# Attention's probabilities turned in pairs of 64-row tiles, and a sign carried by two slopes

## The chip, the cores and the metric

One core of a Trainium2 chip runs one launch that computes attention and two MLP blocks. The metric is the device time of that launch in microseconds (us); the time of a kernel is the median of its runs. Engines: PE is TensorE (PEld its weight loads), DVE is VectorE, ACT is ScalarE, POOL is GpSimd, SP is SyncE, which issues the transfers.

## What is computed

Three stages for 4 batches of 576 tokens, 8 heads of 64 columns, model width 512. Inputs are float32, but the weight matrices of all stages but one (`w_sg`) come as float64.

```python
q_rot, k_rot = (rotate(q), rotate(k))
scores = scale * np.matmul(q_rot, k_rot.transpose(0, 1, 3, 2))
scores = scores - np.max(scores, axis=-1, keepdims=True)
attn = np.exp(scores)
attn = attn / (np.sum(attn, axis=-1, keepdims=True) + 1e-09)
x = np.matmul(attn, v)                      # heads side by side: (4, 576, 512)
xn = (x - mu) / np.sqrt(var + 1e-06) * g_ln # LN over 512
x = x + np.maximum(xn @ w_ch1, 0.0) @ w_ch2 # 512 -> 2048 -> 512
h = gelu(x @ w_in)                          # 512 -> 1024, u and v halves
v_s = np.einsum('ts,bsd->btd', w_sg, norm(v)) + b_sg
out = x + (u * v_s) @ w_out
```

## The kernel before

**Attention** (class `Attn`) goes through 32 blocks: 4 batches (groups `g` 0 to 3), 4 pairs of heads `p`, 2 spans `hi` of queries (0 to 383 and 384 to 575). Group 0 takes all first spans, then all second ones. A block has units of 128 queries for both heads of the pair (3 for span 0; for span 1 one, and one of 64 queries whose two heads share the 128 rows): 80 units, 64 of them full. A unit (`unit`) computes the scores of 576 keys per head: queries and keys of head j lie on partitions 64j to 64j + 63, so the two heads' matmuls use the two 64-row halves of TensorE's array (row tiles). Scores go to PSUM tiles S0 and S1, two banks each. VectorE takes each row's maximum (L293), ScalarE the exponential into `P` in SBUF with the row sums (L303). `turn` transposes `P` with 128x128 transposes (L334), three to a PSUM tile `T` of one bank (two such tiles, tag `T`), nine for a full unit and five for one of 64 queries; `evac` copies each tile into `PT` on ACT or DVE (L347; L352 and L356 for the unit of 64 queries). When a whole block is turned, `values` multiplies with v: one full-array matmul for the last 64 keys of both heads (L394) and eight with 64 output columns each, a pair on the two column halves of the array (column tiles, L398). Then the reciprocal row sums are transposed (L408), copied and multiplied in. PV, these reciprocals and the LN sums (L508) use the tag `T` too.

**MLP.** Each group's LN and MLP (`ln`, `rest`, `up`, `down`) run on TensorE in between the attention of later groups: rounded high and low words in fp32r, three matmuls of 288 columns per 128x128 block (L655 to L657 up, L685 to L687 down), PSUM tag `m` with two banks. The third stage (`moe2`, PSUM tag `p`) follows and is not touched.

**Weights.** `double_parts` turns 44 tiles of float64 (128x512) into float32: ACT scales the high word as a float (L54) and the low word (L56), DVE shifts and joins them (L58) and then joins in the sign bit (L60). `convert` (32 tiles of the first MLP) and `split` (12 of the third stage) call it.

**Order.** Within an engine the instructions stand in program order, and that is set by a planner (`Sched`): tasks name an engine, an earliest time and a duration; the one that could start first goes next, and one of a lower rank may go ahead if it could start within `HOLD` of the duration. Ranks (`UNIT`, `RANK`, `NORM`, `REST`) are tables by group, `EVEN` sets how copies are shared between ACT and DVE. Each engine runs its list in order, so a waiting instruction holds up all behind it.

Of the kernel before, what the change touches and what calls it, by code (L numbers as in the profile page):

```python
# [15 lines left out]
HQ = 288  # L16
# [6 lines left out]
HOLD = 0.2  # L23
UNIT = [2, 1, 3, 2.5]
EVEN = [0, 9, 3, -1]
RANK = dict(turn=4.5, evac=1.25, values=2.25, end=-1, convert=2.75, prep=3.5, load=4, loader=4)
NORM, REST = [2.25, 0, 3.5, 1.25], [0.25, 4.5, 1, 1]
# [15 lines left out]
def double_parts(nc, q, pool, src, bufs):  # L43
# [10 lines left out]
    nc.scalar.activation(f32(e), f32(H), AF.Copy, scale=2.0 ** -112)  # L54
# [4 lines left out]
    yield None  # L59
    nc.vector.scalar_tensor_tensor(e, H, -0x80000000, e, op0=ALU.bitwise_and, op1=ALU.bitwise_or)  # L60
# [3 lines left out]
class Sched:  # L64
# [7 lines left out]
    def __init__(self):  # L72
        self.e = dict.fromkeys(("PE", "DVE", "ACT", "POOL", "SP"), 0.0)
        self.tasks = []
        self.n = 0

# [6 lines left out]
    def go_on(self, t, end):  # L83
        try:
            t["eng"], t["at"], t["us"], *rank = t["gen"].send(end)
# [49 lines left out]
class Attn:  # L135
# [10 lines left out]
    def __init__(self, tc, ctx, k, groups, sched):  # L146
# [5 lines left out]
        self.T, self.qin, self.kin, self.vfree, self.K = Bank(2), Bank(QB), Bank(2), Bank(2), Bank(KB)  # L152
# [105 lines left out]
    def unit(self, i):  # L258
# [3 lines left out]
        x0 = (g, B["p"])  # L262

        heads = range(2 if m == 128 else 1)
        for n in range(2):
            yield "PE", (lambda: latest(*self.Sfree, Kb["k"], B["q"], self.k["x0_free"](*x0))) if n == 0 else 0.0, 0.57
# [5 lines left out]
            self.Sfree = [None, None]  # L272
        e = c.e["PE"]
        if u["t"] == 0:
            self.k["x0"](*x0)
        if u["last"]:
            self.qin.give(B["qslot"], e + 0.1)
            if B["hi"]:
                self.QD.give(B["dslot"], e + 0.1)
            Kb["kusers"] -= 1  # L280
            if Kb["kusers"] == 0:
                self.K.give(Kb["kslot"], e + 0.1)
        if i + 1 < len(self.units):
            c.task(self.unit(i + 1), UNIT[self.units[i + 1]["g"]])
        if u["t"] == 0:
            self.ahead(B["n"])
            B["su"] = self.p.tile([128, 6], F32, tag="su", name="su", bufs=3)
            B["left"] = 0
        at = []
        nb = self.p.tile([128, 2], F32, tag="nb", name="nb", bufs=3)  # L290
        for j in heads:
            e = yield "DVE", e + 0.35 if j == 0 else 0.0, 0.77
            nc.vector.tensor_reduce(nb[:, j:j + 1], S[j], AX.XY, ALU.max, negate=True)  # L293
            at.append(e + 0.1)
        P = None
        u["P"] = []
        for j in heads:
            e = yield "ACT", (lambda: latest(at[0], self.P.free())) if j == 0 else at[j], 0.97
            if j == 0:
                slot = self.P.take()  # L300
                P = self.p.tile([128, 1152], F32, tag="P", name="P", bufs=PB)
# [4 lines left out]
            if len(heads) == 1:  # L306
                self.Sfree[1] = e + 0.05
            if j == 0:
                c.task(self.turn(u, P, slot, at), RANK["turn"])
            if len(heads) == 1:  # L310
# [3 lines left out]
        if u["last"]:  # L314
            c.task(self.scale(B, e + 0.15), RANK["values"])

    def turn(self, u, P, slot, at):

        nc, c, B, q0, m = self.nc, self.c, u["B"], u["q0"], u["m"]
        full = m == 128  # L320
        for k in range(3 if full else 2):
            need = 1 if full and k else 0
            e = yield "PE", (lambda: latest(u["P"][need] if len(u["P"]) > need else None, self.T.free(),
                                            0.0 if B["pt"] else self.PT.free())), 0.39
# [3 lines left out]
            bank = self.T.take()  # L328
            ps = self.ps.tile([128, 512], F32, tag="T", name="T", bufs=2)
            for i in range(3 * k, 3 * k + 3):  # L330
                if not full and i > 4:
                    break
                n = i - 3 * k
                nc.tensor.transpose(ps[:, 128 * n:128 * n + 128], P[:, 128 * i:128 * i + 128], self.k["ident"])  # L334
            c.task(self.evac(u, k, ps, bank, e, full), RANK["evac"])
            B["left"] += 1
        self.P.give(slot, e + 0.1)
        u["turned"] = True

    def evac(self, u, k, ps, bank, e, full):  # L340
        nc, c, B, q0 = self.nc, self.c, u["B"], u["q0"]
# [3 lines left out]
        if full:  # L345
            e = yield eng, e + 0.35, 0.52
            copy(t[:, 3 * k:3 * k + 3, q0:q0 + 128], ps[:, 0:384].rearrange("p (c q) -> p c q", c=3))  # L347
        else:
            for j in range(2):
                a, n = 5 * j + 3 * k, (3, 1)[k]  # L350
                e = yield eng, e + 0.35 if j == 0 else 0.0, (0.33, 0.2)[k]
                copy(t[:, a:a + n, q0:q0 + 64], ps[:, 0:128 * n].rearrange("p (c j q) -> p c j q", c=n, j=2)[:, :, j, :])  # L352
            for j in range(2) if k else ():
                r = slice(64 * j, 64 * j + 64)
                e = yield eng, 0.0, 0.2
                copy(t[r, 4, q0:q0 + 64], ps[r, 128 + 64 * j:192 + 64 * j])  # L356
        self.T.give(bank, e + 0.1)
        B["left"] -= 1
        B["ready"] = max(B.get("ready", 0.0), e + 0.1)
        u["out"] = u.get("out", 0) + 1  # L360
        if u["last"] and u["out"] == 1:
            c.task(self.values(B, u), RANK["values"])
# [19 lines left out]
    def values(self, B, u):  # L382
# [5 lines left out]
        ready = lambda: B["ready"] if u.get("turned") and B["left"] == 0 else None  # L388
        for s in range(2):
            e = yield "PE", (lambda: latest(ready(), self.T.free(), V["v"])) if s == 0 else 0.0, 0.15 + 0.00168 * n * (3, 2)[s]  # L390
            if s == 0:
                bank = self.T.take()
                ps = self.ps.tile([128, 512], F32, tag="T", name="PV", bufs=2)
# [10 lines left out]
        f = yield "PE", lambda: latest(B.get("inv"), self.T.free()), 0.08 + 0.00087 * n  # L404
        b2 = self.T.take()
        pb = self.ps.tile([128, 512], F32, tag="T", name="inv", bufs=2)
# [4 lines left out]
        self.T.give(bank, e + 0.1)  # L411
# [8 lines left out]
        self.T.give(b2, e + 0.1)  # L420
# [21 lines left out]
def fused_kernel(ctx, tc, q, k, v, cs, cst, w12, wi, wo, wsg, wsg4, gb, out):  # L442
# [36 lines left out]

    attn_ctx = ExitStack()  # L480
# [650 lines left out]
```

## Time and profile before

| | |
|---|---|
| time, median of 3 runs | 948.84 us (948.66 to 951.78) |
| the profiled execution | 947.07 us, span 945.3 us |
| PE busy | 916.1 us, 97% |
| PEld busy | 799.5 us, 85% |
| DVE busy | 638.3 us, 68% |
| ACT busy | 490.9 us, 52% |
| chain that ended last | PE 93%, DVE 3%, ACT 2%, DMA 1%, issue 1% |
| granted TensorE clock over the span | 1.000 |

The profile is of one execution. Busy shares count an engine's instructions from start to end; TensorE's overlap, so what a matmul costs in a stream is read from the distance between starts. Attention's transposes lie between 15 and 539 us of the span; the first MLP matmul starts at 89.84 us.

### The profile page before, as it was taken

The page shows a single profiled execution, that of the slowest core. Times are in us where ns is not written, and L with a number is a line of the kernel's source. Part 1 is how long each engine was busy: PE and PEld are TensorE (multiplying, and loading weights), DVE is VectorE, ACT ScalarE, POOL GpSimd, SP SyncE. Part 2 cuts the span into 40 slices and gives each one's busy share as a digit, 9 for nine tenths or more (in the row PEclk, how much of TensorE's full clock was granted, in tenths as well). Part 3 has the DMA queues.
Part 4 walks back from the last instruction along what each step waited for, and adds up shares of the span by engine and source line. Part 5 has one row for each costly group of instructions (what it writes and reads, how often), then busy time and mean ns, then how long its engine had stood idle before and what let it go on. Part 6 is the DMA issues. An engine that isn't in the chain of part 4 may idle for free.

```text
span 945.3 us, 16622 instructions
## 1 busy us (share of the span) xinstructions
PE 916.1 (97%) x6448; PEld 799.5 (85%) x6448; DVE 638.3 (68%) x1353; ACT 490.9 (52%) x1191; POOL 0.8 (0%) x9
## 2 busy tenths in 40 slices
PE   4889999999999999999999999989999999999998
PEld 2446878788788787899877899989999999999998
DVE  6799887887869744825767423674534898676754
ACT  2688787778654755524255413444322656263530
POOL 0000000000000000000000000000000000000000
PEclk9999999999999999999999999999999999999999
DMA  6477616674536055225730453878752201202011
GB/s 205 167 239 242 218 43 199 220 249 172 201 110 206 18 182 182 84 74 184 230 114 22 131 163 98 304 238 295 247 190 80 84 1 31 83 1 88 1 51 51
DMA packets 57791, 134.69 MB, mean 142 GB/s; under 512 B 8048, under 2 KB 30448, under 8 KB 57712
## 3 DMA queue, kind: packets, MB, share of 16 engines
q1 hardware_dynamic: 56880, 132.96, 42.5%
q8 instruction: 51, 0.84, 0.4%
q10 hardware_dynamic: 832, 0.66, 0.3%
q14 instruction: 28, 0.23, 0.1%
HBM read 106.50 MB, written 26.21 MB: 140 GB/s over the span
## 4 chain that ended last, share of the span: by engine, by line
PE 93%; DVE 3%; ACT 2%; DMA 1%; issue 1%; SPq 0%; DVEq 0%
PE S L271 9%; PE T L334 8%; PE m L686 7%; PE m L685 7%; PE m L687 7%; PE m L655 7%; PE PV L398 7%; PE m L656 7%; PE m L657 7%; PE PV L394 2%; PE p L964 2%; PE p L962 2%; PE p L963 2%; PE p L1062 2%; PE p L1046 2%; PE p L1061 2%
## 5 line engine op out<-in xcount | busy, mean ns | idle before, releaser
L655 PE MATMUL m<-xh,w 128*128 128x288 f32 x480 | 147.1, 306 | 3.5 <-DVE h L665 3.5
L685 PE MATMUL m<-h,w 128*128 128x288 f32 x480 | 146.0, 304 | 0.0
L686 PE MATMUL m<-h,w 128*128 128x288 f32 x480 | 141.8, 295 | 0.0
L656 PE MATMUL m<-xl,w 128*128 128x288 f32 x480 | 141.6, 295 | 0.0
L657 PE MATMUL m<-xh,w 128*128 128x288 f32 x480 | 141.2, 294 | 0.0
L687 PE MATMUL m<-h,w 128*128 128x288 f32 x480 | 140.5, 293 | 0.0
L303 ACT ACTIVATE P<-S,nb 128x576 f32<-128x576 f32 x144 | 106.4, 744 | 42.4 <-DVE nb L293 39.3
L665 DVE SCALAR_TENSOR_TENSOR h<-m,h 128x288 fp32r<-128x288 f32 x128 | 58.1, 455 | 100.5 <-ACT h L663 99.4
L293 DVE TENSOR_REDUCE nb<-S 128x1 f32<-128x576 f32 x144 | 103.6, 752 | 26.4 <-PE S L271 25.8
L334 PE MATMUL T<-ident,P 128*128 128x128 f32 x656 | 100.1, 280 | 9.0 <-ACT P L303 4.9
L347 ACT COPY PT<-T 128x384 f32<-128x384 f32 x157 | 70.7, 483 | 69.4 <-PE T L334 69.2
L334 PEld LDWEIGHTS T<-ident,P 128*128 128x128 f32 x656 | 74.9, 141 | 37.3 <-issue 12.7
L663 ACT ACTIVATE h<-m 128x288 fp32r<-128x288 f32 x128 | 52.5, 410 | 100.2 <-PE m L657 98.7
L271 PE MATMUL S<-K,qin 64*128 64x288 f32 x512 | 85.2, 439 | 11.0 <-DVE K L205 11.0
L655 PEld LDWEIGHTS m<-xh,w 128*128 128x128 f32 x480 | 90.1, 188 | 5.8 <-DVE h L665 4.2
L685 PEld LDWEIGHTS m<-h,w 128*128 128x128 f32 x480 | 90.1, 188 | 0.8 <-DVE acc L709 0.4
L686 PEld LDWEIGHTS m<-h,w 128*128 128x128 f32 x480 | 90.4, 188 | 0.4
L656 PEld LDWEIGHTS m<-xl,w 128*128 128x128 f32 x480 | 90.3, 188 | 0.2
L657 PEld LDWEIGHTS m<-xh,w 128*128 128x128 f32 x480 | 90.3, 188 | 0.0
L687 PEld LDWEIGHTS m<-h,w 128*128 128x128 f32 x480 | 90.1, 188 | 0.0
L271 PEld LDWEIGHTS S<-K,qin 64*128 64x128 f32 x512 | 47.7, 190 | 31.1 <-DVE K L205 11.0
L398 PE MATMUL PV<-PT,vin 128*64 128x384 f32 (+1 forms) x512 | 70.3, 413 | 0.0
(148 smaller groups left out, 1797.3 us busy)
## 6 DMA issues: line engine op xcount, KB each, us to landing
w<-wsc SPq DMA_DIRECT2D x96, 512.0 KB, 4.0
cd<-in_w SPq DMA_DIRECT2D x32, 512.0 KB, 4.3
wsc<-w SPq DMA_DIRECT2D x24, 512.0 KB, 4.2
kin<-in_k SPq DMA_DIRECT2D x15, 576.0 KB, 5.9
vin<-in_v SPq DMA_DIRECT2D x20, 320.0 KB, 3.9
qin<-in_q SPq DMA_DIRECT2D x16, 384.0 KB, 5.2
x1d<-x SPq DMA_DIRECT2D x32, 144.0 KB, 3.3
x<-x1d SPq DMA_DIRECT2D x32, 144.0 KB, 2.8
```

The source lines that it names most:

```text
L271: nc.tensor.matmul(S[j][:, n, :], q, Kb["K"][r, a:a + HQ], start=True, stop=True)
L293: nc.vector.tensor_reduce(nb[:, j:j + 1], S[j], AX.XY, ALU.max, negate=True)
L303: nc.scalar.activation(P[:, 576 * j:576 * j + 576].rearrange("p (n k) -> p n k", n=2), S[j], AF.Exp, bias=nb[:, j:j + 1], scale=1.0, accum ...
L334: nc.tensor.transpose(ps[:, 128 * n:128 * n + 128], P[:, 128 * i:128 * i + 128], self.k["ident"])
L347: copy(t[:, 3 * k:3 * k + 3, q0:q0 + 128], ps[:, 0:384].rearrange("p (c q) -> p c q", c=3))
L398: nc.tensor.matmul(ps[r, 0:n], V["vin"][:, ch, r], t[:, 5 * j + ch, 0:n], start=False, stop=ch == 3, skip_group_check=True)
L655: nc.tensor.matmul(ps, w[:, 0, ms], xh[:, kc, :], start=kc == 0, stop=False)
L656: nc.tensor.matmul(ps, w[:, 0, ms], xl[:, kc, :], start=False, stop=False)
L657: nc.tensor.matmul(ps, w[:, 1, ms], xh[:, kc, :], start=False, stop=kc == 3)
L685: nc.tensor.matmul(ps, w[:, 0, ms], t[:, 0, :], start=a == 0, stop=False)
L686: nc.tensor.matmul(ps, w[:, 1, ms], t[:, 0, :], start=False, stop=False)
L687: nc.tensor.matmul(ps, w[:, 0, ms], t[:, 1, :], start=False, stop=a == n - 1)
```

## The change

- **Transposes.** `turn` works on a block's list of 64-row by 128-key pieces: for each 128 keys of a unit it issues two transposes of 64 queries, one on each row half of the array, into the two banks of one PSUM tile `T` (`[128, 2, 512]`, one such tile in place of two small ones). Eight such pairs fill it (four and five in the blocks `ALONE`); a group may span units. `evac` copies a unit's part of a group in one instruction.
- **Scores.** In the blocks `ALONE` (batch 0, first span, four blocks) a unit is done for head 0, then for head 1, each waiting for its own S tile only.
- **Values.** The fifth chunk (last 64 keys) becomes a column pair like the others; PV and the reciprocals share one `T`, and in batch 0's first span use `m`'s PSUM tiles. The LN sums get 128 output columns in place of 64.
- **Sign.** ACT's pass over the high word is Prelu with scale 2^-112 for positive words and 2^-112 times 2^32 for negative ones: the shift by three puts that power on the sign bit. DVE's sign step goes, 44 times.
- **Planner.** It adds `SWITCH` when TensorE's tiling changes; the tables of ranks are others.

```diff
@@
-HOLD = 0.2
...
+HOLD = 0.3
+SWITCH = 0.2
+ALONE = ((0, 0),)
...
@@
-    nc.scalar.activation(f32(e), f32(H), AF.Copy, scale=2.0 ** -112)
+    nc.scalar.activation(f32(e), f32(H), AF.Prelu, scale=2.0 ** -112, alpha=2.0 ** 32)
...
     nc.vector.scalar_tensor_tensor(e, e, 3, d[:, :, 0], op0=ALU.logical_shift_left, op1=ALU.bitwise_or)
-    yield None
-    nc.vector.scalar_tensor_tensor(e, H, -0x80000000, e, op0=ALU.bitwise_and, op1=ALU.bitwise_or)
     yield f32(e)
@@
+            if t["eng"] == "PE":
+                if t["mode"] != self.mode:
+                    t["us"] += SWITCH
+                self.mode = t["mode"]
@@
-    def turn(self, u, P, slot, at):
...
-            bank = self.T.take()
-            ps = self.ps.tile([128, 512], F32, tag="T", name="T", bufs=2)
-            for i in range(3 * k, 3 * k + 3):
...
-                nc.tensor.transpose(ps[:, 128 * n:128 * n + 128], P[:, 128 * i:128 * i + 128], self.k["ident"])
+    def turn(self, B, units):
...
+        blocks = [(u, i) for u in units for i in range(9 if u["m"] == 128 else 5)]
...
+            cuts.append(min(cuts[-1] + (8 if (B["g"], B["hi"]) not in ALONE else 5 if i or u["m"] < 128 else 4), len(blocks)))
...
+            self.T.take()
+            ps = self.ps.tile([128, 2, 512], F32, tag="T", name="T")
...
+            for n, (x, i) in enumerate(some):
+                for j in range(2):
+                    r = slice(64 * j, 64 * j + 64)
+                    nc.tensor.transpose(ps[:, j, 64 * n:64 * n + 64], x["tile"][r, 128 * i:128 * i + 128], self.k["ident"][r, r])
@@
-            copy(t[:, 3 * k:3 * k + 3, q0:q0 + 128], ps[:, 0:384].rearrange("p (c q) -> p c q", c=3))
+                copy(t[:, i:i + n, q0:q0 + 128].rearrange("p c (j q) -> p j c q", j=2),
+                     ps[:, :, 64 * s:64 * s + 64 * n].rearrange("p j (c q) -> p j c q", q=64))
@@
-                nc.tensor.matmul(ps[:, 0:n], V["vin"][:, 4, :], t[:, 4, 0:n], start=True, stop=False, skip_group_check=True)
-            for ch in (2 * s, 2 * s + 1):
...
+            for ch in chs:
                 for j in range(2):
                     r = slice(64 * j, 64 * j + 64)
-                    nc.tensor.matmul(ps[r, 0:n], V["vin"][:, ch, r], t[:, 5 * j + ch, 0:n], start=False, stop=ch == 3, skip_group_check=True)
+                    nc.tensor.matmul(ps[r, 0:n], V["vin"][:, ch, r], t[:, 4 if ch == 4 else 5 * j + ch, 0:n], start=ch == 0, stop=ch == 4)
@@
-            nc.tensor.matmul(ps, ones[:, 0:m], x, start=i == 0, stop=i == len(xs) - 1)
+            nc.tensor.matmul(ps, ones, x, start=i == 0, stop=i == len(xs) - 1)
```

How TensorE's list begins, before (S_79 and S_80 are the two heads' score tiles; a row with x3 stands for three instructions):

```order
L271 MATMUL S_79<-K,qin 128x288
L271 MATMUL S_80<-K,qin 128x288
L271 MATMUL S_79<-K,qin 128x288
L271 MATMUL S_80<-K,qin 128x288
L334 MATMUL T<-ident,P 128x128 x3
L271 MATMUL S_79<-K,qin 128x288
L271 MATMUL S_80<-K,qin 128x288
```

and now:

```order
L281 MATMUL S_79<-K,qin 128x288 x2
L281 MATMUL S_80<-K,qin 128x288 x2
L281 MATMUL S_79<-K,qin 128x288 x2
L281 MATMUL S_80<-K,qin 128x288 x2
L353 MATMUL T<-ident,P 128x64 x8
L281 MATMUL S_79<-K,qin 128x288 x2
L353 MATMUL T<-ident,P 128x64 x10
```

The two heads no longer alternate: a head's two matmuls stand together, and its transposes follow in groups of four and five pairs.

TensorE in the middle of the MLP (m) of group 0, beside the attention of group 1, before:

```order
L657 MATMUL m<-xh,wx 128x288
L271 MATMUL S_79<-K,qin 128x288
L271 MATMUL S_80<-K,qin 128x288
L271 MATMUL S_79<-K,qin 128x288
L271 MATMUL S_80<-K,qin 128x288
L334 MATMUL T<-ident,P 128x128 x6
L655 MATMUL m<-xh,wx 128x288
L656 MATMUL m<-xl,wx 128x288
L657 MATMUL m<-xh,wx 128x288
```

and now, at about the same place:

```order
L281 MATMUL S_79<-K,qin 128x288
L281 MATMUL S_80<-K,qin 128x288
L281 MATMUL S_79<-K,qin 128x288
L281 MATMUL S_80<-K,qin 128x288
L726 MATMUL m<-h,w 128x288
L727 MATMUL m<-h,w 128x288
L728 MATMUL m<-h,w 128x288
L726 MATMUL m<-h,w 128x288
L727 MATMUL m<-h,w 128x288
L728 MATMUL m<-h,w 128x288
L353 MATMUL T<-ident,P 128x64 x12
L726 MATMUL m<-h,w 128x288
```

Six transposes stood right behind the scores, on the full array like the MLP; now the scores are followed by the MLP, and six pairs of transposes (x12) stand by themselves between MLP matmuls.

## Rows read from the trace of the kernel before

**Rows 1.** The table by stretches: busy us and instructions by engine, clock, DMA.

```profile
core 0: us, PE busy (x) PEld busy (x) DVE busy (x) ACT busy (x) POOL busy (x), PEclk, DMA share, GB/s
11.00:90.00 79.00, 68.53 (x380) 40.56 (x381) 69.58 (x138) 57.25 (x136) 0.00 (x0) 1.00 0.59 197
90.00:525.00 435.00, 433.58 (x3134) 360.52 (x3134) 314.68 (x659) 262.32 (x675) 0.00 (x0) 1.00 0.45 151
```

**Rows 2.** The timeline, PE: start, us, engine, line, operation, out<-in, shapes, count.

```profile
89.26 0.82 PE L334 MATMUL T<-ident,P 128*128 128x128 f32 x6
89.84 0.38 PE L655 MATMUL m<-xh,w 128*128 128x288 f32 x1
90.05 0.29 PE L656 MATMUL m<-xl,w 128*128 128x288 f32 x1
...
90.58 0.29 PE L657 MATMUL m<-xh,w 128*128 128x288 f32 x1
```

**Rows 3.** The timeline, PE, 101.1 to 103.4 us: scores and transposes between MLP matmuls.

```profile
101.18 0.29 PE L657 MATMUL m<-xh,w 128*128 128x288 f32 x1
101.41 1.24 PE L271 MATMUL S<-K,qin 64*128 64x288 f32 x8
102.58 0.77 PE L334 MATMUL T<-ident,P 128*128 128x128 f32 x5
103.10 0.38 PE L685 MATMUL m<-h,w 128*128 128x288 f32 x1
103.31 0.29 PE L686 MATMUL m<-h,w 128*128 128x288 f32 x1
```

**Rows 4.** The timeline, PE, 95.2 to 97.4 us: the values of a block.

```profile
95.24 0.48 PE L394 MATMUL PV<-PT,vin 128*128 128x192 f32 x2
95.65 1.52 PE L398 MATMUL PV<-PT,vin 128*64 128x192 f32 x16
97.10 0.44 PE L408 MATMUL inv<-ident,rb 128*128 128x128 f32 x2
97.38 1.14 PE L271 MATMUL S<-K,qd 128*128 128x288 f32 x4
```

**Rows 5.** The timeline, PE, of two ever longer stretches: score passes merged.

```profile
301.88 0.76 PE L271 MATMUL S<-K,qin 64*128 64x288 f32 x4
301.88 1.00 PE L271 MATMUL S<-K,qin 64*128 64x288 f32 x6
```

**Rows 6.** The timeline, PEld, of short stretches: weight loads merged, scores' and transposes'.

```profile
301.88 0.19 PEld L271 LDWEIGHTS S<-K,qin 64*128 64x128 f32 x2 [0.17 <-issue]
301.88 0.30 PEld L271 LDWEIGHTS S<-K,qin 64*128 64x128 f32 x4 [0.17 <-issue]
303.05 0.20 PEld L334 LDWEIGHTS T<-ident,P 128*128 128x128 f32 x2 [0.39 <-issue]
```

**Rows 7.** The timeline, PEld and PE, of short stretches from 53.3 us on.

```profile
53.38 0.14 PEld L334 LDWEIGHTS T<-ident,P 128*128 128x128 f32 x1 [0.22 <-ACT P L303]
53.41 0.30 PE L334 MATMUL T<-ident,P 128*128 128x128 f32 x1
53.38 0.20 PEld L334 LDWEIGHTS T<-ident,P 128*128 128x128 f32 x2 [0.22 <-ACT P L303]
```

**Rows 8.** The timeline, 38.9 to 46 us: a unit of the first stage.

```profile
39.03 1.47 PE L271 MATMUL S<-K,qin 64*128 64x288 f32 x8
...
40.31 1.41 DVE L293 TENSOR_REDUCE nb<-S 128x1 f32<-128x576 f32 x2
...
41.55 0.55 PE L334 MATMUL T<-ident,P 128*128 128x128 f32 x3 [0.24 <-ACT PT L347]
...
42.84 0.77 ACT L303 ACTIVATE P<-S,nb 128x576 f32<-128x576 f32 x1
```

**Rows 9.** Groups by line: count, busy us, mean ns, idle us before, releasers.

```profile
L334 PE MATMUL T<-ident,P 128*128 128x128 f32 x656 | 100.1, 280 | 9.0 <-ACT P L303 4.9 <-DVE PT L347 2.2 <-ACT PT L347 1.5
L60 DVE SCALAR_TENSOR_TENSOR ce<-cd,ce 128x512 int32<-128x512 int32 x44 | 30.3, 688 | 0.8
L347 ACT COPY PT<-T 128x384 f32<-128x384 f32 x157 | 70.7, 483 | 69.4 <-PE T L334 69.2
```

More of the change, by code (lines that the diff above doesn't have):

```diff
@@ L22 @@
 L_CONV = 10.0
-HOLD = 0.2
[L24 to L27, printed above, removed]
+HOLD = 0.3
+SWITCH = 0.2
+ALONE = ((0, 0),)
+UNIT = [0.5, 2, 2.75, 4]
+EVEN = [3, 3, -3, 3]
+RANK = dict(end=-1, convert=2.75, prep=2.75, load=4.5, loader=0.75)
+NORM, REST = [-1, 1, 2.25, 1], [1.75, 0.75, 1.5, 4.5]
+TURN, EVAC, VAL = [0.75, 1.5, 0, 2.75], [0.25, 0, 1.75, 3.5], [1.75, -1, 2.25, 3]
 FG = [4, 8, 8, 4]
@@ L256, in load_v, with unit @@
             self.c.task(v_task(), RANK["load"] + 0.02 * bi)
-    def unit(self, i):
+    def unit(self, i, heads=None):
         nc, c, u = self.nc, self.c, self.units[i]
@@ L262, in unit @@
         x0 = (g, B["p"])
-        heads = range(2 if m == 128 else 1)
+        if heads is None:
+            heads = (0, 1) if m == 128 and (g, B["hi"]) not in ALONE else (0,)
+        single = m == 64
         for n in range(2):
-            yield "PE", (lambda: latest(*self.Sfree, Kb["k"], B["q"], self.k["x0_free"](*x0))) if n == 0 else 0.0, 0.57
+            yield "PE" if single else "PEr", (lambda: latest(*(self.Sfree[j] for j in ((0, 1) if single and (g, B["hi"]) not in ALONE else heads)), Kb["k"], B["q"],
+                                                             self.k["x0_free"](*x0))) if n == 0 else 0.0, 0.49
             for j in heads:
@@ L283, in unit @@
[L283 to L290, printed above, removed]
+        if heads[0] == 0:
+            if u["t"] == 0:
+                self.k["x0"](*x0)
+                self.ahead(B["n"])
+                B["su"] = self.p.tile([128, 6], F32, tag="su", name="su", bufs=3)
+                B["left"] = 0
+                B["turned"] = False
+            u["P"], u["at"] = [], []
+            u["nb"] = self.p.tile([128, 2], F32, tag="nb", name="nb", bufs=3)
@@ new lines, in unit @@
+        after = single or heads[-1] == 1
+        if not after:
+            c.task(self.unit(i, (1,)), UNIT[g])
+        if after:
+            if u["last"]:
+                self.qin.give(B["qslot"], e + 0.1)
+                if B["hi"]:
+                    self.QD.give(B["dslot"], e + 0.1)
+                Kb["kusers"] -= 1
+                if Kb["kusers"] == 0:
+                    self.K.give(Kb["kslot"], e + 0.1)
+            if i + 1 < len(self.units):
+                c.task(self.unit(i + 1), UNIT[self.units[i + 1]["g"]])
@@ L305, in unit @@
             self.Sfree[j] = e + 0.05
[L306 to L310, printed above, removed]
+            if j == 0 and u["t"] == 0:
+                c.task(self.turn(B, [x for x in self.units if x["B"] is B]), TURN[B["g"]])
+            if single:
                 e = yield "ACT", 0.0, 0.2
@@ L313, in unit @@
             u["P"].append(e + 0.15)
-        if u["last"]:
-            c.task(self.scale(B, e + 0.15), RANK["values"])
-    def turn(self, u, P, slot, at):
[L319 to L324, printed above, removed]
+        if after and u["last"]:
+            c.task(self.scale(B, e + 0.15), VAL[B["g"]])
+    def turn(self, B, units):
+        nc, c = self.nc, self.c
+        blocks = [(u, i) for u in units for i in range(9 if u["m"] == 128 else 5)]
+        cuts = [0]
+        while cuts[-1] < len(blocks):
+            u, i = blocks[cuts[-1]]
+            cuts.append(min(cuts[-1] + (8 if (B["g"], B["hi"]) not in ALONE else 5 if i or u["m"] < 128 else 4), len(blocks)))
+        for v, z in zip(cuts, cuts[1:]):
+            some = blocks[v:z]
+            u, i = some[-1]
+            need = 1 if u["m"] == 128 and i > 3 else 0
+            e = yield "PEr", lambda: latest(u["P"][need] if len(u.get("P", ())) > need else None, self.T.free(),
+                                            0.0 if B["pt"] else self.PT.free()), 0.06 * len(some)
             if not B["pt"]:
@@ L555, in rest @@
         r = G[g, "r"]
-        nc.scalar.copy(r[a:a + m], ps)
+        nc.scalar.copy(r[a:a + m], ps[a:a + m])
         mpsb.give(bank, e + 0.05)
@@ L627, in convert @@
         next(parts)
-        yield "DVE", e + 0.1, 0.7
-        next(parts)
-        e = yield "DVE", 0.0, 0.7
+        e = yield "DVE", e + 0.1, 0.7
         s = next(parts)
@@ L880, in split @@
             next(parts)
-            for at in (e + 0.1, 0.0):
-                e = yield "DVE", at, 0.7
-                s = next(parts)
+            e = yield "DVE", e + 0.1, 0.7
+            s = next(parts)
             cdb.give(slot, e)
```

129 lines of the change are left out of this document (71 added, 58 removed).

## The prediction

> **What bounds the kernel now.** I read the table by stretches first: it says which engine is full in which stage. From 90 to 525 us TensorE is busy 433.6 of 435 us while VectorE has 314.7 and ScalarE 262.3 [rows 1]: there the program ends when TensorE's list of work ends, and only a shorter list, or a new hole in it, moves the end. After that stretch attention is all but over and the change touches little. From 11 to 90 us it is another regime: 68.5 of 79 us on TensorE, 69.6 on VectorE, 57.3 on ScalarE [rows 1]; no engine is full, and a unit goes round a chain.
>
> Busy time of TensorE counts overlapped work twice, so I take prices from the distance between starts, in the timeline. Six transposes and the MLP matmul behind them take 89.26 to 90.05, 0.79 us; an MLP matmul alone steps by 0.13 (four of them from 90.05 to 90.58), so a 128x128 transpose costs 0.11 us [rows 2], 0.109 in what follows. All 656 of them [rows 9] cost some 71.5 us. Next I read what it costs to enter a split array. From 101.18 to 103.31 stand two MLP steps (0.27), eight score passes that run two by two on the two 64-row halves (four steps of 0.24 [rows 5], 0.97) and five transposes (0.55): 1.79 us of work in 2.13 us, so one visit to row tiles costs about 0.34 us on top of its work [rows 3]. For column tiles: from 95.24 to 97.38, 2.14 us, stand two passes over 192 columns, eight pairs of such passes and two transposes [rows 4]; at the scores' rate of 0.24 us for 288 columns a pass or pair takes 0.16, so this is 1.82 us of work and 0.32 us for the visit.
>
> **The change, part by part.**
>
> *Transposes in pairs.* 656 transposes of 128 rows become 656 pairs of 64-row transposes, each with 64 moving columns in place of 128. Nothing in the trace is a paired transpose, so I bound it. The stream: a pair of score passes takes 0.24 us for 288 columns, from the growth of the merged rows by 0.24 [rows 5]; 64 columns would be 0.053 us. The weights: in row tiles the loads of both halves start together (two loads take 0.19 us, no more than one) and the next two start 0.11 later [rows 6]; a transpose's load is quicker: one takes 0.14 us, two 0.20, so the second starts 0.06 after the first [rows 6, 7]. If a half's transpose loads like the whole one, a pair costs 0.057 to 0.06. Two things could make it dearer. Its load could be as long as a score's, 0.11; or the four instructions of a pair could come no faster than TensorE's sequencer hands them out. Where the engine had been empty and waited for ACT, load, matmul and next load came at 53.38, 53.41 and 53.44 [rows 7]: about 0.029 us each, so 0.116 for a pair. I take 0.06: where the engine had not been empty, four loads and two matmuls of the scores started within 0.11 us or little more from 301.88 on [rows 5, 6], faster than 0.029 each, and most groups stand behind scores or MLP work. Ends: 0.057 and 0.116.
>
> A rule of the Trainium skill speaks against this part: "TensorE: Matmul & The Clock Gate", section "LDWEIGHTS (loading the stationary operand)", says that a load takes columns / 1.2 ns whatever the number of rows. By it a pair of 128-column loads takes at least 0.107 us, and nothing would be won by splitting rows. The trace agrees for the scores (0.11) and not for transposes (0.06 from load to load). By the rule the sum below would come to 954 us (947.1 - 656 x 0.002 + 8.0), by the rows to 931.
>
> 525 of the 656 lie behind 90 us (131 before it, counted in the trace). 525 x (0.109 - 0.060) = 25.7 us less.
>
> *More visits.* Before, transposes run on the full array next to the MLP, at no price. Now they need row tiles. Counted over the whole order from the first MLP matmul on: row-tile visits go from 50 to 81 (49 of them begin with transposes alone), column-tile visits from 33 to 26, since the LN sums lose their 64 columns and the values' fifth chunk moves into the column pairs. A visit that starts with transposes has the shorter load, one that ends in MLP the longer: 0.32 to 0.37, I take 0.33. +31 x 0.33 = 10.2, -7 x 0.32 = -2.2: 8.0 us more. So this stage gets 25.7 - 8.0 = 17.7 us shorter.
>
> *The values' fifth chunk* goes from one full matmul to a column pair, which by the same rate takes as long (0.16 for 192 columns) [rows 4]: nothing.
>
> *One PSUM tile T of two banks in place of two tiles.* A group of eight pairs is copied out in one piece of up to 1024 columns. The 384-column copy takes 0.483 us on ACT [rows 9]; for 1024 I estimate 1.0 to 1.3. With the two hand-overs, estimated at 0.25 us each (TensorE stood 0.24 us for such a copy [rows 8]), T comes back 1.5 to 1.8 us after its last transpose. Behind a waiting transpose stand MLP matmuls that could have run, and ACT and DVE wait for those. In the order, 109 times another use of T follows in this stage, mostly with 6 to 24 MLP matmuls between (0.8 to 3.2 us); 20 of them stand nearer than 1.5 us, short by 7.7 us together, and measured against 1.8 us the shortage is 14 us. Before, such waits for PT copies came to 3.7 us in the whole program [rows 9]. Several of the near ones follow the values, where only a multiply is still due. I take 4 us, ends 0 and 14.
>
> *VectorE's sign step.* 44 x 0.688 = 30.3 us go from VectorE [rows 9]. Cover: behind 90 us VectorE is at 72% beside a full TensorE, so this is worth nothing there; were it the bound, it would be worth at most those 30. Prelu in place of Copy is still one ACT pass over the same 512 columns, and the order has 19 table loads before and after; a dearer Prelu would sit under ScalarE's cover (60% in that stretch). The PSUM copies, counted in the orders, fall from 288 to 192 with the same columns: also covered.
>
> *The first stage.* For the first four blocks (12 units) a unit now computes one head's scores, then the other's. Alone, a head uses one half of the array: its four passes of 0.24 take as long as both heads' did, so TensorE pays up to 12 x 0.97 = 11.7 us more. It saves 131 x 0.049 = 6.4 us on transposes. Against that stands the chain: scores at 39.03, maxima at 40.31, the second exponential from 42.84 for 0.77 us [rows 8], and the next scores need both S tiles; by head, the next scores wait for one exponential. VectorE also loses about ten of its 44 sign steps here (counted up to 100 us), 7 us. The stage lies between -10 us (VectorE's remaining 62.6 us decide) and +5 us (TensorE's list decides and its holes stay). I take -3.
>
> **Sum.** The profiled execution took 947.07 us, a span of 945.3 and 1.8 around it; the median of the runs is 1.8 above that. 947.1 - 17.7 + 4 - 3 = 930.4. I say 931 us, a little towards the median.
>
> **Rivals.**
>
> *A pair is no cheaper than the transpose it replaces (0.11 to 0.116): slower.* The price of the visits is then left over. At 0.11: 947.1 + 656 x 0.001 + 8.0 = 956 us; at 0.116: 947.1 + 4.6 + 8.0 = 960 us. It decides from 0.094 us a pair on, where 525 x (0.109 - p) equals 8.0. This is also the case where the change doesn't do what it says, two halves that take turns (2 x 0.057). For it: the hand-out at 0.029 per instruction. Against: score passes pair, and the groups stand behind MLP work. (The Trainium skill's load rule ends just below this rival's lower end.)
>
> *The one T tile becomes the stall.* If copies queue behind exponentials (0.77 us each [rows 8]) on ACT and T comes back after 1.8 to 2.2 us, TensorE waits 14 to 25 us in place of 4: 941 to 951 us. For it: the tight places counted above. Against: the waits of before, which were short.
>
> *The first stage gets longer*, as TensorE's extra score time is not hidden: +5 in place of -3, 939 us.
>
> **How the numbers follow.** Forecast 0.66; pairs as dear as before 0.10; T stalls 0.14; longer first stage 0.10. Measurement tells about 0.5% from no change, that is 944 and 954 us. Faster: 0.66 + 0.10 + 0.05 of the T case = 0.81; same: the rest of the T case, 0.09; slower: 0.10. The low end takes 0.057 a pair (19.3 us), -10 in the first stage and no waits: 918, and I add the 1.8 of the median. The high end, 946, takes in the longer first stage and a third of the T case; the pair rival and the worst of the T stalls stay out.
>
> **What would show it.** In the timeline behind 90 us, a group of eight pairs between MLP matmuls should take 0.48 us plus about 0.3 for the visit; 0.9 or more would be the first rival. The row of T's matmuls should show almost no idle time for PT copies; 10 us or more there would be the second. The first MLP matmul stood at 89.84 us before [rows 2]; about 87 is forecast, 95 would be the third. VectorE should lose 30 us of busy time and the end should not notice. I am wrong altogether if TensorE is no longer full behind 90 us.

## The result, and the profile of the changed kernel

The changed kernel takes 939.65 us (median of four runs, 938.12 to 940.02) against 949.35 us for the kernel before on the same chip: a ratio of 0.989, 95% interval 0.9869 to 0.9912. It is faster by about 10 us, where 18 were forecast. The profiled execution took 938.12 us with a span of 936.3, against the 947.07 and 945.3 on which the sum was made.

The table by stretches, as in [rows 1]:

```profile
core 0: us, PE busy (x) PEld busy (x) DVE busy (x) ACT busy (x) POOL busy (x), PEclk, DMA share, GB/s
11.00:90.00 79.00, 72.81 (x522) 46.53 (x522) 54.30 (x107) 54.47 (x124) 0.00 (x0) 1.00 0.45 152
90.00:525.00 435.00, 431.91 (x3733) 353.24 (x3735) 318.30 (x668) 254.16 (x593) 0.00 (x0) 1.00 0.50 166
```

Behind 90 us TensorE is nearly as full as before (431.9 of 435 us, 433.6 before), so there the time still follows its list. Ahead of 90 us it has become fuller, 72.8 us in place of 68.5, and VectorE emptier, 54.3 in place of 69.6.

To see where the time went I followed fixed points of TensorE's list in both traces:

| point of the list | before | after | difference |
|---|---|---|---|
| first score matmul | 11.0 us | 11.8 us | +0.8 |
| last score pass of batch 0's first span | 63.2 | 64.5 | +1.3 |
| first MLP matmul | 89.8 | 93.0 | +3.1 |
| 2000th MLP matmul (of 3072; attention is over) | 582.1 | 575.4 | -6.7 |
| end of the span | 945.3 | 936.3 | -9.0 |

So the start lost 3 us, the stage of MLP beside attention won 9.9, and the rest won another 2.2. Of the 3 us, 0.8 lie ahead of the first score matmul; in a second profile of the changed kernel that matmul stood at 11.2 and the first MLP matmul at 93.8.

**A group of pairs.** The timeline of TensorE (start, us, line, operation, shapes, count) where eight pairs stand alone between MLP matmuls:

```profile
123.39 0.29 PE L728 MATMUL m<-h,w 128*128 128x288 f32 x1
123.61 0.71 PE L353 MATMUL T<-ident,P 64*128 64x64 f32 x16
124.25 0.41 PE L726 MATMUL m<-h,w 128*128 128x288 f32 x1
124.49 0.30 PE L727 MATMUL m<-h,w 128*128 128x288 f32 x1
```

From 123.39 to 124.49 are 1.10 us. Two MLP steps are 0.27; from pair to pair the starts lie 0.062 us apart (median over pairs that follow another pair), so eight are 0.50; that leaves 0.34 for the visit. The forecast was 0.060 and 0.33.

**A visit in which scores and transposes alternate:**

```profile
110.01 0.29 PE L728 MATMUL m<-h,w 128*128 128x288 f32 x1
110.24 0.76 PE L281 MATMUL S<-K,qin 64*128 64x288 f32 x4
110.83 0.54 PE L353 MATMUL T<-ident,P 64*128 64x64 f32 x12
111.19 0.71 PE L281 MATMUL S<-K,qin 64*128 64x288 f32 x4
111.83 0.40 PE L726 MATMUL m<-h,w 128*128 128x288 f32 x1
112.07 0.29 PE L727 MATMUL m<-h,w 128*128 128x288 f32 x1
```

From 110.01 to 112.07 are 2.06 us: two MLP steps (0.27), four score steps (0.97) and six pairs (0.37) make 1.61, and 0.45 is left. Over the visits between MLP matmuls the medians are 0.34 for transposes alone (22 visits), 0.40 for scores alone (4), 0.40 for scores and transposes with one change between them (18) and 0.45 with two changes (17). Before, scores that led to transposes on the full array left 0.35 (24 such visits, the one in [rows 3] among them).

**Transposes that wait for T.** Behind scores on the full array the transposes find T still taken by the values of the block before:

```profile
105.30 1.24 PE L281 MATMUL S<-K,qd 128*128 128x288 f32 x4 [0.50 <-ACT P L318]
107.00 0.71 PE L353 MATMUL T<-ident,P 64*128 64x64 f32 x16 [0.47 <-DVE x L458]
107.64 0.40 PE L696 MATMUL m<-xh,w 128*128 128x288 f32 x1
```

This is the worst of ten such places, nine groups of transposes and one LN sum (TensorE idle 0.47 us until VectorE's multiply; 0.18 or 0.19 us in the other nine). In the whole program TensorE's idle time ahead of transposes stays small, as the page's groups show (busy us, mean ns; idle before and what ended it; the rows that answer to [rows 9]):

```profile
L377 ACT COPY PT<-T 128x512 f32<-128x512 f32 (+6 forms) x99 | 61.1, 634 | 38.5 <-PE T L353 38.1
L353 PE MATMUL T<-ident,P 64*128 64x64 f32 x1312 | 73.8, 234 | 3.6 <-DVE x L454 1.5
```

**The end of the start**, against [rows 2]:

```profile
84.78 1.24 PE L281 MATMUL S<-K,qin 64*128 64x288 f32 x8
86.48 0.71 PE L353 MATMUL T<-ident,P 64*128 64x64 f32 x16 [0.47 <-DVE xc L555]
88.31 0.59 PE L353 MATMUL T<-ident,P 64*128 64x64 f32 x12 [1.11 <-ACT PT L377]
90.17 1.85 PE L435 MATMUL PV<-PT,vin 128*64 128x192 f32 x20 [1.28 <-ACT PT L388]
...
92.98 0.51 PE L696 MATMUL m<-xh,w 128*128 128x288 f32 x1
```

Three pauses in a row, for LN's subtraction and for two copies out of T: no MLP matmul is ready yet to stand in them.

### The profile page after: what moved, and what is told of

It is laid out like the page before. It is cut to its first block, busy times and chain, and to the rows that moved or that the text cites. A ratio compares the mean times of both kernels' runs of the same rounds, so it can differ in the third digit from the quotient of the medians.

```text
span 936.3 us, 17850 instructions
## 1 busy us (share of the span) xinstructions
PE 911.1 (97%) x7168; PEld 789.7 (84%) x7168; DVE 614.7 (66%) x1305; ACT 481.1 (51%) x1099; POOL 0.8 (0%) x9
## 4 chain that ended last, share of the span: by engine, by line
PE 94%; ACT 2%; DVE 2%; DMA 1%; issue 1%; SPq 0%; DVEq 0%
PE S L281 10%; PE PV L435 9%; PE m L726 8%; PE m L696 8%; PE m L727 7%; PE m L728 7%; PE m L698 7%; PE m L697 7%; PE T L353 6%; PE p L1004 2%; PE p L1002 2%; PE p L1003 2%; PE p L1101 2%; PE p L1102 2%; PE p L1085 2%; PE p L1084 2%
## 5 line engine op out<-in xcount | busy, mean ns | idle before, releaser
L281 PE MATMUL S<-K,qin 64*128 64x288 f32 x512 | 106.1, 459 | 14.7 <-DVE K L212 11.8
L704 ACT ACTIVATE h<-m 128x288 fp32r<-128x288 f32 x128 | 52.5, 410 | 106.9 <-PE m L698 106.0
L435 PE MATMUL PV<-PT,vin 128*64 128x384 f32 (+1 forms) x640 | 88.7, 419 | 1.3 <-ACT PT L388 1.3
L281 PEld LDWEIGHTS S<-K,qin 64*128 64x128 f32 x512 | 55.9, 201 | 34.8 <-DVE K L212 11.8
L353 PEld LDWEIGHTS T<-ident,P 64*128 64x128 f32 x1312 | 59.8, 143 | 28.1 <-issue 9.1
L377 ACT COPY PT<-T 128x512 f32<-128x512 f32 (+6 forms) x99 | 61.1, 634 | 38.5 <-PE T L353 38.1
L353 PE MATMUL T<-ident,P 64*128 64x64 f32 x1312 | 73.8, 234 | 3.6 <-DVE x L454 1.5
```

The costliest lines, as they stand in the source:

```text
L281: nc.tensor.matmul(S[j][:, n, :], q, Kb["K"][r, a:a + HQ], start=True, stop=True)
L353: nc.tensor.transpose(ps[:, j, 64 * n:64 * n + 64], x["tile"][r, 128 * i:128 * i + 128], self.k["ident"][r, r])
L377: copy(t[:, i:i + n, q0:q0 + 128].rearrange("p c (j q) -> p j c q", j=2), ps[:, :, 64 * s:64 * s + 64 * n].rearrange("p j (c q) -> p j c q ...
L435: nc.tensor.matmul(ps[r, 0:n], V["vin"][:, ch, r], t[:, 4 if ch == 4 else 5 * j + ch, 0:n], start=ch == 0, stop=ch == 4)
```

## The experiments

Times are medians of three rounds. The kernel before took 948.38 us beside four of them (full transposes, without head by head, and the first two of the sign step), 947.42 beside the other eight. The first and the 2000th MLP matmul are the fixed points of the table above; where a difference is split at them, it is by the profiles, against the second profile of the changed kernel.

**The changed kernel once more**, as the base for the others.

> The changed kernel itself, once more, on the chip of the runs beside it. 938 to 941 us if the 939.65 us of its first runs is its time on any chip; 944 or more if the first chip was kinder to it, and then the 947 to 948 us of the changed kernel with the sign step put back, and without the head-by-head blocks, would be no loss.

Measured: 939.12 us (938.69 to 939.77), ratio 0.9907 (0.9881 to 0.9933). The first MLP matmul stood at 93.8 us. So 939.1 is what the runs below are held against; for the four whose kernel before ran 1 us slower, differences of that size mean nothing.

### What the pairs bring

Full 128-row transposes in place of pairs, with the order held:

```diff
-for j in range(2):
-    r = slice(64 * j, 64 * j + 64)
-    nc.tensor.transpose(ps[:, j, 64 * n:64 * n + 64], x["tile"][r, 128 * i:128 * i + 128], ident[r, r])
+nc.tensor.transpose(ps[:, n // 4, 128 * (n % 4):128 * (n % 4) + 128], x["tile"][:, 128 * i:128 * i + 128], ident)
...   # the copies read T as one row of 128-column pieces
```

> The changed kernel with its order held, but each pair of 64-row transposes is one 128-row transpose on the full array into the same PSUM tile. Theory (a pair steps by 0.062 us, a full transpose by 0.109, and a visit to row tiles costs 0.34): between the first and the 2000th MLP matmul the work grows by 520 x 0.047 = 24 us, the 32 visits of transposes alone go (-11 to -14 us), so this stretch grows by 10 to 13 us; the first stage by 0 to 6; in all 949 to 958 us. Rival 1 (visits cost next to nothing): 24 to 31 us more, 963 to 971 us. Rival 2 (the pairs gain nothing and the one T tile is what costs): 940 us or less.

Measured: 972.12 us (970.59 to 972.84), ratio 1.0259 (1.0244 to 1.0275): 33.0 us above the changed kernel. The first MLP matmul came 12.2 us later (106.0), the stage of MLP beside attention took 20.3 us more. The time lies just above the range of the case in which visits cost next to nothing (963 to 971). The timeline, TensorE:

```profile
110.18 1.09 PE L351 MATMUL T<-ident,P 128*128 128x128 f32 x8
111.03 0.38 PE L694 MATMUL m<-xh,w 128*128 128x288 f32 x1
```

Eight full transposes behind scores take 0.85 us to the next start, 0.106 each, where eight pairs take 0.50. So the pair is the gain the forecast took it for, and the first rival (a pair as dear as a transpose) is out. Visits need not be cheap for that. The expectation took 32 of them to go; in the trace they fall from 107 to 96 in the full stage, and 520 transposes at 0.047 (24.4 us) less 11 visits at 0.34 are 20.7 us, where 20.3 were measured. In the start 136 transposes at 0.047 are 6.4 us, and 12.2 were lost. TensorE stood idle no longer there than with pairs (16.3 us up to the first MLP matmul, 11.1 of them ahead of the first score matmul; 16.9 and 11.2 with pairs), and the granted clock fell by about as much in both profiles (0.66 and 0.92 in two stretches of 4 us from 100 us on here, 0.84 and 0.73 from 87 us on with pairs); but full transposes between scores make its list change tiling 65 times in place of 37.

### What a visit costs

64 extra transposes of one 64-row half, each ahead of an MLP sum and overwritten by it; nobody waits for them:

```diff
 for kc in (2 * s, 2 * s + 1):   # ahead of this loop, in up()
+if g < 2:
+    nc.tensor.transpose(ps[:, 0:64], ident[0:64, :], ident[0:64, 0:64])
```

> The changed kernel with 64 extra single transposes of 64 rows put ahead of MLP sums of groups 0 and 1, one each, written where the sum then starts; the order is held and nobody waits for them. About 47 of them stand between full-array work and open a visit to row tiles of their own, the others lengthen one. If a bare visit costs 0.30 to 0.40 us: 47 x 0.33 to 0.43 with the transpose, 15 to 20 us more, 954 to 960 us. If the price read from the trace is mostly waits around real visits and a bare one costs 0.1 or less: 943 to 946 us.

Measured: 958.39 us (956.79 to 959.62), 19.3 us more. The timeline, TensorE:

```profile
100.13 0.29 PE L700 MATMUL m<-xh,w 128*128 128x288 f32 x1
100.35 0.27 PE L695 MATMUL m<-ident 64*128 64x64 f32 x1
100.55 0.40 PE L698 MATMUL m<-xh,w 128*128 128x288 f32 x1
100.79 0.30 PE L699 MATMUL m<-xl,w 128*128 128x288 f32 x1
```

From 100.13 to 100.79 are 0.66 us where two MLP steps are 0.27: one transpose in a visit of its own costs 0.39. 48 of the 64 stand so, the other 16 lengthen a visit; 19.3 us over 48 is 0.40, a little high, since the 16 are in it. A visit's price is its own and not that of waits around it.

Groups of at most four pairs in place of eight (the planner makes a new order):

```diff
-cuts.append(min(cuts[-1] + (8 if (B["g"], B["hi"]) not in ALONE else 5 if i or u["m"] < 128 else 4), len(blocks)))
+cuts.append(min(cuts[-1] + (4 if (B["g"], B["hi"]) not in ALONE else 5 if i or u["m"] < 128 else 4), len(blocks)))
```

> The changed kernel with groups of at most four pairs in place of eight (the four blocks of the first span of batch 0 stay as they are); the order is made anew. By the list, visits to row tiles between the MLP matmuls go from 81 to 143. If a visit costs 0.40 us wherever it stands: 62 x 0.40 = 25 us more, less a few us from a shorter hold of T: 958 to 966 us. If what matters is the hold and not the visits: 936 to 944 us.

Measured: 970.81 us (967.7 to 971.02), 31.7 us more. This is above the first case's range. Between the first and the 2000th MLP matmul 167 visits in place of 107, and 29.0 us longer: 0.48 for each added one, waits and a fall of the granted clock (0.85 from 140 to 150 us) counted in. The groups of eight, which run over a unit's end, are as much a part of the gain as the pairs: with four, the change would be slower than the kernel before.

The planner told a price of 0.4 per change of tiling:

```diff
-SWITCH = 0.2
+SWITCH = 0.4
```

> The changed kernel with the planner's price of a change of tiling at 0.4 in place of 0.2, the price of a bare visit by the run with 64 extra ones; the order is made anew and has 78 visits to row tiles in place of 81. 3 x 0.4 = 1.2 us less, 937 to 939 us, if the number of visits is all that moves; 940 to 945 us if the tables of ranks fit the old price and the new order opens waits elsewhere.

Measured: 944.99 us (944.35 to 945.88), 5.9 us more, so the second case. From the first to the 2000th MLP matmul it is 0.8 us shorter with three visits fewer (1.0 at 0.34 each), but the first MLP matmul comes at 101.5 us: a truer price for the full stage made a worse start. Part of that is the clock (below).

### The one T tile

T given back earlier after the values: ScalarE copies the turned reciprocals out, VectorE multiplies from SBUF.

```diff
+if not early:
+    e = yield "ACT", f + 0.25, 0.13 + 0.001 * (n if B["hi"] == 0 else 256)
+    rs = B["rb"].rearrange("p a b -> p (a b)")
+    nc.scalar.copy(rs[:, 0:n if B["hi"] == 0 else 256], pb[:, 0:n if B["hi"] == 0 else 256])
+    pb = rs
+    self.T.give(0, e + 0.1)
...
 if early:
     ...
-else:
-    self.T.give(0, e + 0.1)
```

> The changed kernel with the one T tile given back earlier after the values: ScalarE copies the turned reciprocals out to SBUF, VectorE multiplies from there, so that transposes no longer wait for VectorE's multiply (in the trace the visits behind the 64-query scores cost 0.60 us in place of 0.35, twelve of them). If that hold costs: 3 to 5 us less, 934.5 to 937 us. If the hold only moves to the next release, or the 32 more ScalarE copies come in the way: 938 to 943 us.

Measured: 938.45 us (937.14 to 938.68), 0.7 us less: no difference to speak of. TensorE's weight loads of transposes had waited 4.8 us for VectorE's multiply between 93 and 525 us; now they wait 7.5 us for ScalarE's new copy. The hold moved to the next release.

The copy out of T shared by both engines:

```diff
-e = yield eng, at, us(128 * n)
-copy(t[:, i:i + n, q0:q0 + 128]..., ps[:, :, 64 * s:64 * s + 64 * n]...)
+for j in range(2):
+    f = yield ("ACT", "DVE")[j], at, (0.2 + 0.00074 * 64 * n, 0.15 + 0.00105 * 64 * n)[j]
+    e = max(e, f)
+    (nc.scalar.copy, nc.vector.tensor_copy)[j](t[:, i:i + n, q0 + 64 * j:q0 + 64 * j + 64], ps[:, j, 64 * s:64 * s + 64 * n]...)
```

> The changed kernel with each group's copy out of the one T tile shared: ScalarE copies the first bank, VectorE the second, at the same time, so T should come back some 0.4 us earlier after a group of eight. The planner is told and the order made anew. If the hold of T is what the start lost (TensorE waits 4 to 6 us for copies before 93 us): the first MLP matmul at 90 us or earlier and 934 to 937 us. If the release is set by when VectorE and ScalarE get to the copy, or the second copy's own cost eats the gain: 940 to 946 us.

Measured: 951.58 us (949.87 to 952.02), 12.5 us more, outside both cases; 4.3 us of it lie ahead of the first MLP matmul, 8.7 between it and the 2000th. What TensorE waited for from 11 to 105 us (total, times, longest), in the changed kernel and then here:

```profile
PE S L281 <- ACT P L318: 2.5, 3, 1.5
PE PV L435 <- ACT PT L388: 1.3, 1, 1.3
PE T L353 <- ACT PT L377: 1.1, 1, 1.1
```

```profile
PE T L353 <- DVE PT L379: 7.4, 9, 1.5
PE S L281 <- ACT P L318: 2.6, 3, 1.5
```

Each half is shorter, but T is free only when the later engine is done, and VectorE gets to its half late: 7.4 us of waits in place of 1.1. VectorE is not full (busy 24.8 of 30 us from 50 to 80), but the sharing also gives it more to do: its copies out of T take 63 us in the whole program, where they took 27. The run doesn't tell these two apart.

### Head by head in the start

Without it:

```diff
-ALONE = ((0, 0),)
+ALONE = ()
```

> The changed kernel with no block done head by head (ALONE is empty, groups of eight pairs everywhere). Theory (head by head, the scores use half of the array, and that eats what the pairs save in the first stage): TensorE's score time in the first stage falls by up to 11 us and the first MLP matmul comes between 3 us earlier and 3 us later, 936 to 943 us. Rival (head by head is what breaks the chain of scores, maximum and exponentials): the first MLP matmul comes 6 us later or more, 945 us and up.

Measured: 948.51 us (947.64 to 950.66), ratio 1.0006 (0.9992 to 1.0021): 9.4 us more; 4.8 us lie ahead of the first MLP matmul (98.5), 3.9 between it and the 2000th. The stretch from 11 to 63 us, before, changed, and without it:

```profile
11.00:63.00 52.00, 44.53 (x239) 25.41 (x240) 43.90 (x77) 34.19 (x81) 0.00 (x0) 1.00 0.53 174
```

```profile
11.00:63.00 52.00, 49.10 (x307) 32.35 (x308) 34.09 (x60) 30.36 (x67) 0.00 (x0) 1.00 0.33 113
```

```profile
11.00:63.00 52.00, 39.43 (x290) 26.08 (x292) 34.88 (x60) 33.35 (x73) 0.00 (x0) 0.97 0.53 183
```

and what TensorE waits for there (11 to 65 us) without it:

```profile
PE S L281 <- ACT P L318: 9.0, 5, 1.9
PE T L353 <- ACT PT L377: 3.5, 3, 1.2
```

With both heads at once TensorE is busy 39 of 52 us and waits for ScalarE to give back score tiles and T; the last score pass of the span comes at 72.0 us. Head by head it is busy 49 us, and the same pass comes at 64.5. But the kernel before had reached it at 63.2, with both heads at once and its two T tiles. So with one T tile, its longer copies and the new tables the chain got some 9 us longer, and head by head buys back 7.5 of that at this point, 5 at the first MLP matmul; nothing is left over. Which of the three weighs most was not isolated: a version with two large T tiles was not tried. Nor is all of the 9 us the waits themselves: the granted clock of this run was 0.54 from 60 to 64 us and 0.61 to 68, which can be up to 3 us of them (an estimate: TensorE's busy time there times the missing share).

Without it, and with the shared copy (the diffs of this and the run before together):

> The changed kernel without head-by-head blocks (948.5 us alone) and with the copy out of T shared by both engines as in the run beside it. If the first stage got 9 us longer without head-by-head blocks because ScalarE's long copies out of T stand in its chain: 940 to 944 us, the first MLP matmul back from 98.5 to 93 or 94 us. If the chain is held by the scores' own hand-overs (maximum, exponential, two S tiles): 947 to 951 us.

Measured: 977.57 us (976.12 to 979.43), 29.1 us more than without head by head alone; the first MLP matmul at 113.0 us. It fell outside both cases. Scores wait 11.0 us for exponentials up to 65 us, transposes 3.9 for VectorE's copies, and the granted clock is 0.79 from 50 to 80 us and 0.78 from there to 110. So putting half of each copy on VectorE made the start longer, not shorter. Whether ScalarE's long copies are the cause stays open, since the run adds work to VectorE as well, and the clock fell.

### The sign step

The kernel before with the new sign (Prelu, no VectorE step) and nothing else:

```diff
-nc.scalar.activation(f32(e), f32(H), AF.Copy, scale=2.0 ** -112)
+nc.scalar.activation(f32(e), f32(H), AF.Prelu, scale=2.0 ** -112, alpha=2.0 ** 32)
...
-nc.vector.scalar_tensor_tensor(e, H, -0x80000000, e, op0=ALU.bitwise_and, op1=ALU.bitwise_or)
```

> The kernel before with only the sign part of the change: Prelu on ACT, VectorE's sign step gone, all else in the same order. Theory (cover): 947 to 950 us, VectorE's busy time 30 us lower. Rival (VectorE at 88% bounds the first stage): the first MLP matmul comes 3 to 7 us earlier, 942 to 946 us.

Measured: 947.64 us (946.13 to 951.29), ratio 0.9989 (0.9968 to 1.001): nothing, as the forecast had it.

The changed kernel with the old sign, order held (the diff above, the other way round):

> The changed kernel with VectorE's sign step put back 44 times and Copy in place of Prelu, every other instruction in the same order. Theory (the step had cover): VectorE's busy time rises by 30 us and the time stays that of the changed kernel, 938 to 941 us. Rival (VectorE's relief shortened the first stage, where its busy time from 11 to 90 us fell from 69.6 to 54.3): the first MLP matmul comes 3 to 7 us later and the time is 943 to 947 us.

Measured: 947.34 us (946.36 to 947.8), ratio 0.9995 (0.9986 to 1.0005): 8.2 us more, nearly the whole gain of the change (2.1 us ahead of the first MLP matmul, 4.3 between it and the 2000th, 2.5 behind it). By this the cover was gone. But an order made without the step might be to blame, so once more with the planner told:

```diff
-e = yield "DVE", e + 0.1, 0.7
+yield "DVE", e + 0.1, 0.7
+next(parts)
+e = yield "DVE", 0.0, 0.7
 s = next(parts)
...   # the same in split; double_parts yields between the two steps
```

> The changed kernel with VectorE's sign step back, and this time the planner is told of it (0.7 us each), so that its order is made for it; with the step put back into an order made without it the time was 947.3 us. If that order was the cause (work behind VectorE that the planner thought free): 938 to 942 us. If the 30 us of VectorE work themselves cost (one T tile and the MLP's h wait for VectorE, the start is a chain): 943 to 948 us.

Measured: 942.03 us (939.96 to 942.24), ratio 0.9931 (0.9907 to 0.9955): 2.9 us more by the medians, between the two cases' ranges. So of the 8.2 us some 5 came of an order that didn't know of the step. The 2.9 that stay need not be the step's own: this is another order, with 109 visits in place of 107, and another order alone moved the time by 5.9 us in the run with the planner's other price. Where the step sat in an order that didn't know of it, VectorE's multiplies came late; from 93 to 525 us TensorE waited, in that kernel and then in the changed one:

```profile
PE T L354 <- DVE x L455: 3.5, 8, 1.3
PE m L697 <- DVE h L707: 0.9, 2, 0.7
```

```profile
PE T L353 <- DVE x L454: 1.3, 7, 0.2
```

## Why the prediction was right in sign and short in size

Its sum took 16.7 us off the profiled execution; 9.0 came. By its terms:

| term | forecast | in the traces |
|---|---|---|
| pairs in the full stage | -25.7 | -25.9 |
| visits there | +8.0 | +12.6 |
| waits for the one T there | +4 | +2.8 |
| up to the first MLP matmul | -3 | +3.1 |
| the rest of that stage | 0 | +0.6 |
| behind the 2000th MLP matmul | 0 | -2.2 |
| sum | -16.7 | -9.0 |

*Pairs: right.* The choice of 0.060 between 0.057 and 0.116 stands at 0.062, and undoing it costs 33 us, 20.3 of them in the full stage. (The -25.9 counts the work of the list between the two fixed points at its undisturbed steps, 461.9 us before and 436.0 after; 25.0 of it are transposes, the rest is work that now stands ahead of the first point.)

*Visits: mis-sized.* Between the fixed points are 107 visits in place of 79, 28 more where the sum had 24 (counted by tiling they are 107 in place of 82; before, five of these stood directly behind one another in two places); at 0.34 these four are at most 1.4 us. The price was the larger slip: the sum gave each visit one price, 0.33, and read it from visits of scores that led to transposes on the full array, or of values alone. Now a visit with scores leads to MLP matmuls and mostly holds transposes too, and leaves 0.40 or 0.45 in place of 0.35; by the medians this is some 3 us. Together that is nearly all of the 4.6 us that were missing.

*The one T: right.* The ten places behind full-array scores cost 2.8 us more than a visit alone. (Two long visits with several groups, at 302 and 489 us, cost 1.4 more than others, but the waits that the trace shows in them are for ScalarE's exponentials; they are in the rest of the stage.) The second rival (941 to 951) did not come: 3.6 us of idle time ahead of transposes in the whole program. With shared copies, or with a VectorE step that the order didn't know of, these waits grew (7.4 us in the start, 4.0 between 93 and 525 us). In the two new orders made by the same tables, with the sign step planned and with the planner's other price, they stayed near 2 us behind the start. So it takes an order that fits the copies; whether it takes these tables is not shown.

*The first stage: wrong in sign.* This is the largest miss, 6 us. The step that failed is the one that let the chain get shorter because the next scores would wait for one exponential only. It held the chain of before against the extra score time, and left the single T and its longer copies out of this stage: they were counted for the full stage alone, where MLP matmuls stand between two uses. Up to 93 us there are none, and the chain got longer. That the hold of T is what made it longer is argued and not shown: without head by head TensorE waits 9.0 us for score tiles up to 65 us and 3.5 for T. The run without head by head shows the size, some 9 us (new tables and a fall of the clock included). Head by head then makes TensorE the bound of that stretch (49.1 of 52 us busy), so the time got back is no more than what was lost. The run with full transposes fits this: there the start got longer with TensorE's list, at no more idle time. The third rival (939 us, by TensorE's extra score time) named the right place and a time that came out, from half of the cause.

*The sign step: nothing in the kernel before, at most some 3 us in the changed one if the order knows of it.* The cover was named as VectorE's slack beside a full TensorE. That is right as long as TensorE's list has other work while a VectorE result is late. With one T that VectorE's multiply gives back, and a start whose pauses wait for VectorE, the slack as a share of time says less. Part of the 2.2 us behind the 2000th matmul may hang on this too: with the sign step back that part was 2.5 us longer, 1.3 with the step planned. In the kernel before, taking the step out left that part as it was. (VectorE's busy time in the whole program fell from 638.3 to 614.7 us, not by the 30 of the forecast: other VectorE work grew, its copies out of T by 4 us.)

## What to carry to other kernels

Price a visit to another tiling by what stands in it and by how many there are, not only by what its work saves: here pairs won 26 us, and visits gave 13 back; groups half as long would have lost it all. When a double-buffered tile is made into one larger one, look for the stretch where nothing else can run while it is copied out; it is there that the hold can be dear, even if it costs little in the full stage. And a share of idle time on an engine is not cover as such: ask what the delayed result gives back, and who stands behind that in order.

## What was not expected of the hardware

**TensorE's clock fell in the pauses of the start.** By stretches, 83 to 95 us, the changed kernel and then the one with the sign step put back:

```profile
83.00:87.00 4.00, 3.53 (x32) 2.33 (x30) 3.93 (x10) 3.56 (x8) 0.00 (x0) 1.00 0.61 202
87.00:91.00 4.00, 1.61 (x30) 1.26 (x26) 4.00 (x11) 3.74 (x12) 0.00 (x0) 1.00 0.95 331
91.00:95.00 4.00, 4.00 (x31) 3.22 (x28) 3.52 (x10) 3.50 (x10) 0.00 (x0) 1.00 0.94 325
```

```profile
83.00:87.00 4.00, 2.89 (x16) 1.68 (x14) 3.90 (x11) 3.38 (x8) 0.00 (x0) 1.00 0.71 225
87.00:91.00 4.00, 1.66 (x30) 1.34 (x30) 4.00 (x10) 3.36 (x10) 0.00 (x0) 0.70 0.94 353
91.00:95.00 4.00, 4.00 (x23) 2.79 (x24) 3.24 (x7) 2.81 (x8) 0.00 (x0) 0.50 0.68 251
```

In the second, TensorE had been busy 2.89 of 4 us and then 1.66 of the next 4, in which the clock fell; then it was granted 0.50, the lower of its two levels (1.2 GHz), and the twenty value passes took longer, as its timeline shows:

```profile
90.96 3.47 PE L436 MATMUL PV<-PT,vin 128*64 128x192 f32 x20 [1.22 <-ACT PT L389]
```

3.47 us in place of the 1.85 at 90.17 us in the changed kernel. The kernel with the planner's other price shows a like fall (0.50 from 91 to 95 us, 0.65 to 99), the changed kernel's second profile a shorter one (0.84, then 0.73), with its first MLP matmul 0.8 us later than in the first profile, which has none. In the kernel with full transposes the same twenty passes took 3.27 us (0.66 from 100 to 104 us). So waits in the start cost a second time; how much of the difference between these kernels is the clock was not separated. For the changed kernel the fall is the usual case: over the whole span its four runs were granted 1.000, 0.996, 0.996 and 0.996, and the first, on which the table of terms is made, took 938.1 us, the others 939.5 to 940.0. Of the 49 runs of the kernel before beside the experiments, 36 were granted 0.999 or more.

**A visit's price hangs on what stands in it.** Transposes and scores both use row tiles, and still a visit of transposes alone left 0.34 us, one with scores 0.40, and one in which transposes stand between scores 0.45. One change between the two adds nothing to scores alone, two add 0.05. What in it takes the time (a load that can't start early, or the change of operand) stays open.
